# Attention and routing reordered by hand as a software pipeline, diagonal rows on ScalarE, prefix counts on TensorE

## The chip, the cores and the metric

The kernel runs on one core of a Trainium2 chip. The core has five engines with an instruction queue each, which work in order and wait for each other through semaphores: TensorE (PE, matmuls; its weight loads are listed as PEld), VectorE (DVE), ScalarE (ACT), GpSimd (POOL), and SyncE (SP), which here only issues DMAs. The metric is the device time of one execution, in microseconds (us); lower is better.

## The reference, cut to what matters

Inputs are float32: r, k, v of shape (4, 8, 768, 48) (batch, heads, time, head width), decays w and bonus u of (8, 48), eight expert embeddings, a temperature tau, and expert weights w1 (8, 384, 1024) and w2 (8, 1024, 384).

```
for t in range(768):                        # attention, for each batch and head
    y[t]  = r[t] @ (state + outer(u * k[t], v[t]))
    state = w[:, None] * state + outer(k[t], v[t])
x = y as 3072 rows of 384                   # row = batch * 768 + t, all heads side by side
logits = (x / |x|) @ (emb / |emb|).T / tau  # 8 experts
e = argmax(logits); gate = softmax(logits)[e]
out[row] = gate * (relu(x[row] @ w1[e]) @ w2[e])
```

## The kernel before, in words

The time axis is cut in 6 chunks of 128 steps. A chunk of one batch is a unit: 24 units, taken chunk by chunk, the 4 batches of a chunk in turn. Four units make a group, which is routed together.

For one unit (`attend`, L211 to L275) GpSimd scales K into the padded tile Kpad by powers of the decay (L220), and forms KU, the product K * u * R (L222, L223); VectorE sums KU over each head to diag (L225); GpSimd multiplies V by diag to xd, the diagonal term (L227). TensorE transposes R (L231) and Kpad (L236), two heads at a time, into PSUM; VectorE brings R out, scaled, as RT (L233), and ScalarE brings K out as KT (L238). TensorE multiplies KT by RT for all head pairs (L244); VectorE masks the result to AT (L248). TensorE then sums into one PSUM tile the part from the carried state (L255, not in the first chunk) and AT times V (L258); VectorE adds xd to get the rows X (L264). TensorE makes the new state part (L269, not in the last chunk), VectorE adds it to the state (L273) and GpSimd decays the state (L274). A float32 matmul stands in the trace as two instructions, a transpose as one.

For one group (`route`, L332 to L399) ScalarE squares and sums each X (L345), TensorE transposes X (L348), ScalarE brings it out (L350), and TensorE multiplies it by the embeddings (L352). Some twenty small VectorE instructions find the first maximal expert and the gate. Running counts are made on VectorE (`pre`, L378 to L381), and two small matmuls turn them into each row's place in its expert's list (L383, L384). Then SyncE writes the rows to DRAM (L395), and GpSimd writes each row's number into the list with four indirect DMAs, the scatters (L396). The four write the same tensor, so each waits until the one before has landed.

After the last group, SyncE reads the lists back (L409), GpSimd gathers rows (L422), and for each expert TensorE transposes 512 rows (L438) and runs the two matmuls (L444, L449). This part is the same code in both kernels.

The order of each engine's instructions is not as written: a list scheduler places them by its own cost estimates. All PSUM tiles come from one pool of 8 banks, and tiles such as Kpad rotate among 3 buffers. The experts' embeddings are prepared, and the decays' range is checked (`decays`, with the instruction L150), before the first unit.

Of the kernel before, what the change touches and what calls it, by code (L numbers as in the profile page):

```python
# [9 lines left out]
F32 = mybir.dt.float32  # L10
# [8 lines left out]
N = B * S  # L19
C = 128  # L20
# [12 lines left out]
WAKE = 7  # L33
# [6 lines left out]
def build_first(k):  # L40


    nc, pool = k.nc, k.const
    wc = pool.tile([128, NP], F32, name="wc")
    nc.vector.memset(wc, 1.0)
    with nc.allow_non_contiguous_dma(reason="384 words"):
        for s in range(2):
            q = nc.sync if s == 0 else nc.scalar
            q.dma_start(out=wc[s * DP : s * DP + D, :], in_=k.w.rearrange("(p s) d -> s d p", s=2)[s])
    k.ones = pool.tile([128, 128], F32, name="ones")  # L50
    nc.vector.memset(k.ones, 1.0)
    wide = k.aconst.tile([128, 512], F32, name="wide")
    nc.vector.memset(wide, 1.0)
    ps = k.ps.tile([128, 512], F32, name="ps", tag="ps")
    for _ in range(WAKE):
        nc.tensor.matmul(ps, k.ones, wide, start=True, stop=True)
    k.ident = pool.tile([128, 128], F32, name="ident")
    make_identity(nc, k.ident)

    for lst, name, count in ((k.Rpad, "Rpad", 6), (k.Kpad, "Kpad", 3)):  # L60
        for i in range(count):
            t = k.aconst.tile([128, H, DP], F32, name=f"{name}{i}")
            nc.gpsimd.memset(t[:, :, D:DP], 0.0)
            lst.append(t)
    step = k.aconst.tile([128, NP, C], F32, name="step")
    seed = k.aconst.tile([128, NP, C], F32, name="seed")
    nc.gpsimd.memset(seed, 0.0)
    nc.gpsimd.memset(seed[:, :, 0:1], 1.0)
# [4 lines left out]
    nc.vector.tensor_copy(step, wc[:, :, None].to_broadcast([128, NP, C]))  # L73
    nc.vector.memset(step[:, :, 0:1], 0.0)
    t = k.aconst.tile([128, NP, C], F32, name="wpow")
    flat = lambda a: a.rearrange("q p i -> q (p i)")
    nc.vector.tensor_tensor_scan(flat(t), flat(step), flat(seed), 0.0, ALU.mult, ALU.add)
    mid = k.aconst.tile([128, NP], F32, name="mid")
    nc.vector.reciprocal(mid, t[:, :, C // 2])
    k.rpow = k.aconst.tile([128, NP, C], F32, name="rpow")  # L80
    kp = k.aconst.tile([128, NP, C], F32, name="kp")
    over_i = mid[:, :, None].to_broadcast([128, NP, C])
    nc.vector.tensor_mul(kp, t[:, :, ::-1], over_i)
    ps = k.ps.tile([128, NP, 2, DP], F32, name="ps", tag="ps")
    for p in range(NP):
        nc.tensor.transpose(ps[:, p].rearrange("q s d -> q (s d)"), kp[:, p, :], k.ident)
    k.kpow = k.aconst.tile([128, H, D], F32, name="kpow")
    nc.vector.tensor_copy(k.kpow.rearrange("q (p s) d -> q p s d", s=2), ps[:, :, :, 0:D])
    nc.vector.tensor_mul(k.rpow, t, over_i)
    wC = k.aconst.tile([128, NP], F32, name="wC")  # L90
    nc.vector.tensor_mul(wC, t[:, :, C - 1], wc)
    k.wC = wC[:, :, None].to_broadcast([128, NP, D])
# [10 lines left out]
def build_consts(k):  # L103
# [9 lines left out]
    nc.sync.dma_start(  # L113
        out=k.u_bc.rearrange("p h d -> p (h d)"),
        in_=bass.AP(tensor=k.u.tensor, offset=k.u.offset, ap=[[0, 128], [1, DM]]),
    )
    for b in range(B):
# [7 lines left out]
    k.ebase = numbers(k, "ebase", [128, E], [[N, E]], 0, 0)  # L125
# [8 lines left out]
def empty_lists(k):  # L134
    k.nc.sync.dma_start(out=k.list.rearrange("(p n) o -> p (n o)", p=128), in_=k.none)
    k.nc.vector.memset(k.cum, 0.0)


def decays(k):

    nc, pool = k.nc, k.const
    wrow = k.aconst.tile([1, DM], F32, name="wrow")
    nc.sync.dma_start(out=wrow, in_=k.w.rearrange("(o h) d -> o (h d)", o=1))
# [10 lines left out]
def build_experts(k):  # L154

    nc, pool = k.nc, k.aconst
    emb = pool.tile([E, DM], F32, name="emb")
    nc.sync.dma_start(out=emb, in_=k.emb)
    tau = pool.tile([E, 1], F32, name="tau")
    nc.sync.dma_start(out=tau, in_=bass.AP(tensor=k.tau.tensor, offset=k.tau.offset, ap=[[0, E], [1, 1]]))  # L160
# [8 lines left out]
    ps = k.ps.tile([128, NK, E], F32, name="ps", tag="ps")  # L169
# [19 lines left out]
def load(k, i, other=None):  # L189

    nc = k.nc
    other = other or nc.sync
# [8 lines left out]
    other.dma_start(out=R[:, :, 0:D], in_=of(k.r))  # L201
# [9 lines left out]
def attend(k, i):  # L211
# [4 lines left out]
    K, R, V = k.loaded.pop(i)  # L216
    T = k.state[b]

    Kw = k.Kpad[i % len(k.Kpad)]
    nc.gpsimd.tensor_mul(Kw[:, :, 0:D], K, k.kpow)  # L220
    KU = k.work.tile([128, H, D], F32, name="KU", tag="KU")
    nc.gpsimd.tensor_mul(KU, K, k.u_bc)  # L222
    nc.gpsimd.tensor_mul(KU, KU, R[:, :, 0:D])  # L223
    diag = k.work.tile([128, H], F32, name="diag", tag="diag")
    nc.vector.reduce_sum(diag, KU, axis=AX.X)  # L225
# [3 lines left out]
    rt = k.ps.tile([128, NP, C], F32, name="ps", tag="ps")  # L229
# [4 lines left out]
    kt = k.ps.tile([128, NP, C], F32, name="ps", tag="ps")  # L234
# [5 lines left out]
    at = [k.ps.tile([128, NP, C], F32, name="ps", tag="ps") for _ in range(2)]  # L240
    for p in range(NP):
        for s in range(2):
            rows = slice(s * DP, s * DP + D)
# [386 lines left out]
```

## Time and profile before

| | us |
|---|---|
| median of 3 runs (755.43 to 757.86) | 755.45 |
| the profiled execution | 752.4 |
| its span, first to last instruction | 750.5 |
| first transposes of the first unit start | 29.87 |
| first transposes of the first expert start | 386.27 |
| TensorE busy, share of the span | 86% |
| mean granted TensorE clock, share of full speed | 0.742 |

Start times are counted from the span's start. The profile also says at which clock TensorE ran: 0.50 is 1.2 GHz and 1.00 is 2.4 GHz, its two levels. An engine's idle time is listed with what ended it, as in "[0.68 <-ACT KT L238]": idle for 0.68 us, until the ScalarE instruction of line 238 on tile KT was done. A matmul's end is modelled and includes time in which the next already runs, so that the distance from start to start is the better measure.

### The profile page before, as it was taken

The page shows a single profiled execution, that of the slowest core. Times are in us where ns is not written, and L with a number is a line of the kernel's source. Part 1 is how long each engine was busy: PE and PEld are TensorE (multiplying, and loading weights), DVE is VectorE, ACT ScalarE, POOL GpSimd, SP SyncE. Part 2 cuts the span into 40 slices and gives each one's busy share as a digit, 9 for nine tenths or more (in the row PEclk, how much of TensorE's full clock was granted, in tenths as well). Part 3 has the DMA queues.
Part 4 walks back from the last instruction along what each step waited for, and adds up shares of the span by engine and source line. Part 5 has one row for each costly group of instructions (what it writes and reads, how often), then busy time and mean ns, then how long its engine had stood idle before and what let it go on. Part 6 is the DMA issues. An engine that isn't in the chain of part 4 may idle for free.

```text
span 750.5 us, 6703 instructions
## 1 busy us (share of the span) xinstructions
PE 647.1 (86%) x2536; PEld 460.3 (61%) x2536; DVE 168.0 (22%) x414; ACT 80.8 (11%) x169; POOL 213.3 (28%) x282
## 2 busy tenths in 40 slices
PE   4388897899899899898039999999999999999991
PEld 2378887798798798788024545555454555545450
DVE  3533332323333223324010111202011110202000
ACT  1011110100101101102002010010201011010200
POOL 5653352554344242220240211203031221302010
PEclk8555555555555555557559999999999999999996
DMA  9354654313313210100120333424132333300000
GB/s 184 63 149 107 122 94 119 84 32 64 74 33 64 58 26 11 42 1 1 43 62 0 129 100 105 129 84 140 20 136 87 127 109 105 125 1 31 1 30 5
DMA packets 95565, 54.39 MB, mean 72 GB/s; under 512 B 78558, under 2 KB 90175, under 8 KB 95523
## 3 DMA queue, kind: packets, MB, share of 16 engines
q1 hardware_dynamic: 89410, 44.19, 22.9%
q0 software_dynamic: 4864, 9.48, 4.2%
q8 instruction: 22, 0.36, 0.2%
q10 hardware_dynamic: 1248, 0.20, 0.1%
q14 instruction: 21, 0.16, 0.1%
HBM read 45.86 MB, written 11.13 MB: 76 GB/s over the span
## 4 chain that ended last, share of the span: by engine, by line
PE 75%; issue 9%; DMA 4%; POOL 3%; DVE 2%; ACT 2%; SPq 0%; POOLq 0%; DVEq 0%; ACTq 0%
PE ps L444 23%; PE ps L449 22%; PE ps L258 8%; PE ps L244 5%; PE ps L269 4%; DMA list<-token,posi 3%; PE ps L255 3%; PE ps L352 3%; PE ps L231 2%; PE ps L236 2%; PE ps L348 1%; PE ps L438 1%; ACT KT L238 1%; POOL list L396 1%; DVE AT L248 0%
## 5 line engine op out<-in xcount | busy, mean ns | idle before, releaser
L444 PE MATMUL ps<-xTe,w 128*128 128x512 f32 x384 | 168.9, 601 | 0.4 <-DVE xTe L439 0.4
L449 PE MATMUL ps<-w,hT 128*128 128x384 f32 x512 | 166.4, 486 | 0.0
L449 PEld LDWEIGHTS ps<-w,hT 128*128 128x128 f32 x512 | 97.5, 190 | 69.3 <-issue 3.8
L444 PEld LDWEIGHTS ps<-xTe,w 128*128 128x128 f32 x384 | 73.3, 193 | 91.5 <-issue 84.8
L452 POOL DMA_INDIRECT out_dram<-y,take x32 | 32.4, 1011 | 270.2 <-DVE y L451 266.0
L258 PE MATMUL ps<-V,AT 128*128 128x48 f32 x384 | 85.6, 396 | 6.5 <-DVE AT L248 6.5
L258 PEld LDWEIGHTS ps<-V,AT 128*128 128x128 f32 x384 | 84.7, 323 | 8.0 <-DVE AT L248 8.0
L451 DVE TENSOR_SCALAR y<-ps,G 128x384 f32<-128x384 f32 x32 | 19.8, 618 | 298.5 <-PE ps L449 298.5
L445 ACT ACTIVATE hT<-ps 128x512 f32<-128x512 f32 x64 | 38.2, 597 | 319.6 <-PE ps L444 319.6
L244 PE MATMUL ps<-RT,KT 48*128 48x128 f32 x384 | 49.0, 431 | 16.5 <-ACT KT L238 16.5
L244 PEld LDWEIGHTS ps<-RT,KT 48*128 48x128 f32 x384 | 42.1, 320 | 26.0 <-ACT KT L238 26.0
L220 POOL TENSOR_TENSOR Kpad<-K,kpow 128x384 f32<-128x384 f32 x24 | 23.9, 1000 | 87.4 <-PE ps L269 79.9
L269 PE MATMUL ps<-V,Kpad 128*128 128x96 f32 x160 | 44.2, 437 | 0.0
L248 DVE TENSOR_TENSOR AT<-ps,umask 128x512 f32<-128x512 f32 x48 | 30.9, 686 | 50.5 <-PE ps L244 50.5
L396 POOL DMA_INDIRECT list<-token,posi x24 | 24.3, 1014 | 56.9 <-DMA list<-token,posi 46.6
L422 POOL DMA_INDIRECT G<-xs,take x32 | 32.6, 1017 | 26.0 <-PE ps L444 9.9
L255 PE MATMUL ps<-state,RT 128*128 128x96 f32 x160 | 39.5, 427 | 0.0
L269 PEld LDWEIGHTS ps<-V,Kpad 128*128 128x128 f32 x160 | 38.5, 334 | 0.0
L255 PEld LDWEIGHTS ps<-state,RT 128*128 128x128 f32 x160 | 34.8, 321 | 4.4 <-issue 4.2
L264 DVE TENSOR_TENSOR X<-ps,xd 128x384 f32<-128x384 f32 x24 | 13.4, 558 | 99.4 <-PE ps L258 98.3
L352 PEld LDWEIGHTS ps<-ent,xT 128*128 128x128 f32 x144 | 30.5, 314 | 5.2 <-ACT xT L350 5.1
L352 PE MATMUL ps<-ent,xT 128*128 128x8 f32 x144 | 30.1, 337 | 2.9 <-ACT xT L350 2.8
(113 smaller groups left out, 440.8 us busy)
## 6 DMA issues: line engine op xcount, KB each, us to landing
w<-in_moe_w_dram SPq DMA_DIRECT2D x16, 1536.0 KB
xs<-X SPq DMA_DIRECT2D x24, 192.5 KB
K<-in_k_dram SPq DMA_DIRECT2D x24, 192.0 KB
V<-in_v_dram SPq DMA_DIRECT2D x24, 192.0 KB
Rpad<-in_r_dram SPq DMA_DIRECT2D x23, 192.0 KB
G<-xs,take POOLq DMA_INDIRECT x32, 3.2
out_dram<-y,take POOLq DMA_INDIRECT x32, 2.6
list<-token,posi POOLq DMA_INDIRECT x24, 4.8
```

The lines of the kernel that those rows point to most:

```text
L244: mm(at[s][:, p, :], KT[rows, p, :], RT[rows, p, :], start=True, stop=True)
L248: nc.vector.tensor_mul(a, at[s], k.umask[:, None, :].to_broadcast([128, NP, C]))
L255: mm(pair(y, p), RT[:, p, :], T[:, p, :], start=first, stop=False, skip_group_check=True)
L258: mm(y[:, h, :], AT[h % 2][:, h // 2, :], V[:, h, :], start=first, stop=(h == H - 1), skip_group_check=True,)
L269: mm(st[:, p, :], pair(Kw, p), pair(V, p), start=True, stop=True)
L352: mm(lg[:, b, :], xT[:, m, :], k.ent[:, m, :], start=(m == 0), stop=(m == NK - 1))
L396: nc.gpsimd.indirect_dma_start(out=k.list[:, :], out_offset=IndirectOffsetOnAxis(ap=posi[:, b : b + 1], axis=0), in_=k.token[:, c, b : b + ...
L422: nc.gpsimd.indirect_dma_start(out=G[:, :], out_offset=None, in_=k.xs[:, :], in_offset=IndirectOffsetOnAxis(ap=take, axis=0), bounds_check ...
L444: mm(ps[:, 0:n], w1[:, m, f * 128 : (f + 1) * 128], xT[:, m, 0:n], start=(m == 0), stop=(m == NK - 1))
L445: nc.scalar.activation(hT[:, f, 0:n], ps[:, 0:n], ACT.Relu)
L449: mm(ps, hT[:, f, t * 128 : (t + 1) * 128], w2[:, f, :], start=(f == 0), stop=(f == NF - 1))
L452: nc.gpsimd.indirect_dma_start(out=k.out[:, :], out_offset=IndirectOffsetOnAxis(ap=take, axis=0), in_=y[:, :], in_offset=None, bounds_chec ...
```

## The change

The attention part is put under a manual schedule: each engine now runs its instructions in the order in which they are written. `attend` and `route` are cut into steps, and a new function `attention` writes in iteration i the steps of several units: transposes of unit i+1, scaling for unit i+2, sums of unit i, scores of unit i+1, transposed rows of unit i-1, logits of unit i-2, and for a group the choice of expert and the ranks 3 iterations, and places, row write and scatters 4 iterations after its last unit.

The diagonal rows xd move from one GpSimd instruction to eight ScalarE instructions, one for each head. The running counts on VectorE are replaced by three more small matmuls with the matrix of ones. The experts' embeddings are prepared in iteration 1 and the decays' range is checked in iteration 4, their DMAs issued by ScalarE. Seven wake-up matmuls become 6 before and 4 after the first transposes. The decay powers are made by four short scans, unit 0's Kpad by VectorE. Kpad rotates among 4 buffers, PSUM banks are given out by kind of tile, and a group's rows are one tile, written to DRAM by one DMA.

```diff
+def own_rows(k, i):
+    diag, V = k.diag.pop(i), k.loaded[i][2]
+    for h in range(H):
+        k.nc.scalar.mul(xd[:, h, :], V[:, h, :], diag[:, h : h + 1])
-    nc.gpsimd.tensor_mul(xd, V, diag[:, :, None].to_broadcast([128, H, D]))
...
+def ranks(k, g):
+    g.rank = k.ps.tile([128, B, E], F32, name="rank", tag="st")
+    mm(g.rank, k.umask, g.oh, start=True, stop=False)
+    for b in range(1, B):
+        mm(g.rank[:, b:B, :], k.ones, g.oh[:, 0 : B - b, :], start=False, stop=False, skip_group_check=True)
+    mm(g.rank, k.ones, k.cum[:, None, :].to_broadcast([128, B, E]), start=False, stop=True)
-    for b in range(1, B):
-        nc.vector.tensor_add(pre[:, b, :], pre[:, b - 1, :], oh[:, b - 1, :])
-    mm(rank, k.umask, oh, start=True, stop=False)
-    mm(rank, k.ones, pre, start=False, stop=True)
...
+    for i in range(-1, units + 5):
+        if 0 < i + AHEAD < units:
+            load(k, i + AHEAD)
+        if i in (B, 2 * B):
+            load_weights(k, i // B - 1, k.weights[i // B - 1])
+        whole(places, i - 4)
+        whole(put, i - 4)
+        on(own_rows, i)
+        on(turn, i + 1)
+        on(scaled, i + 2)
+        on(own, i + 1)
+        on(states, i)
+        of_group(squares, i - 1)
+        whole(choose, i - 3)
+        on(sums, i)
+        on(carry, i)
+        on(rows, i)
+        on(scores, i + 1)
+        on(own_sum, i + 1)
+        of_group(turn_rows, i - 1)
+        of_group(logits, i - 2)
+        whole(ranks, i - 3)
+        whole(gates, i - 3)
+        if i == 1:
+            build_experts(k)
+        if i == B:
+            decays(k)
...
+        return self.pool.tile(shape, dtype, name=name, tag=tag, bufs={"tp": 2, "at": 2}.get(tag, 1))
...
+    with ExitStack() as ctx1, tc.manual_schedule():
```

TensorE at the start, before: `kp` is the decay power, `emb` the embeddings, `Rpad` the padded R.

```order
L86 MATMUL ps<-ident,kp 128x128 x4
L171 MATMUL ps<-ident,emb 128x8 x3
L231 MATMUL ps<-ident,Rpad_106 128x128 x4
L236 MATMUL ps<-ident,Kpad_118 128x128 x4
L244 MATMUL ps<-RT,KT 128x128 x8
```

The same place after; `wake` is the result of the wake-up matmuls, which nothing reads.

```order
L84 MATMUL kpT<-ident,kp 128x128 x4
L60 MATMUL wake<-wide,ones 128x512 x4
L252 MATMUL rt<-ident,Rpad_119 128x128 x4
L257 MATMUL kt<-ident,Kpad_111 128x128 x4
L270 MATMUL at<-RT,KT 128x128 x8
```

The embedding transposes no longer stand ahead of the first unit, and four wake-up matmuls do.

TensorE in a unit of a middle chunk, before:

```order
L231 MATMUL ps<-ident,Rpad_116 128x128 x4
L236 MATMUL ps<-ident,Kpad_122 128x128 x4
L244 MATMUL ps<-RT,KT 128x128 x8
L255 MATMUL ps<-state_177,RT 128x96 x4
L258 MATMUL ps<-V,AT_680 128x48
L269 MATMUL ps<-V,Kpad_122 128x96 x3
```

And after, where `rt`, `kt`, `st`, `y`, `at`, `xp`, `lg` are the PSUM tiles of the two transposes, the state part, the sums, the scores, the transposed rows and the logits:

```order
L252 MATMUL rt<-ident,Rpad_119 128x128 x4
L257 MATMUL kt<-ident,Kpad_117 128x128 x4
L287 MATMUL st<-V,Kpad_115 128x96 x4
L317 MATMUL y<-state_195,RT 128x96 x4
L320 MATMUL y<-V,AT_732 128x48
...
L270 MATMUL at<-RT,KT 128x128 x8
L411 MATMUL xp<-ident,X 128x128 x3
L426 MATMUL lg<-ent,xT 128x8 x3
```

Before, the scores (L244) follow the transposes of the same unit; after, the state part and all sums of the unit before stand between the two, and the routing's matmuls are spread over the units.

GpSimd around the scatters of a group, before:

```order
L396 DMA list<-token,posi 24576x1 x2
L223 TENSOR_TENSOR KU<-KU,Rpad_110 128x384
L220 TENSOR_TENSOR Kpad_122<-K,kpow 128x8x48
L227 TENSOR_TENSOR xd<-V,diag 128x384
L274 TENSOR_TENSOR state_175<-state_175,wC 48x4x48 x2
L396 DMA list<-token,posi 24576x1 x2
```

After:

```order
L304 TENSOR_TENSOR state_195<-state_195,wpow 48x4x48 x2
L457 TENSOR_TENSOR ssq<-ssq,half 128x4
L486 DMA list<-token,posi 24576x1 x4
L219 TENSOR_TENSOR Kpad_113<-K,kpow 128x8x48
L227 TENSOR_TENSOR KU<-K,u_bc 128x384
L228 TENSOR_TENSOR KU<-KU,Rpad_121 128x384
```

The four scatters now stand in one block, and the scaling of K for the unit after next (L219) stands behind them.

## Rows read from the trace of the kernel before

**Rows 1.** The page, 40 slices of the span: busy tenths, granted clock in tenths.

```profile
PE   4388897899899899898039999999999999999991
PEclk8555555555555555557559999999999999999996
```

**Rows 2.** Busy time by stretch: length, PE, PEld, DVE, ACT, POOL, clock, DMA share, GB/s.

```profile
10.30:29.80 19.50, 0.35 (x3) 0.35 (x3) 7.63 (x17) 0.62 (x2) 17.07 (x19) 0.55 0.57 118
...
190.90:247.97 57.07, 52.04 (x265) 49.08 (x265) 18.09 (x50) 6.85 (x17) 24.60 (x33) 0.50 0.27 56
...
359.00:386.20 27.20, 0.28 (x1) 0.17 (x1) 0.41 (x2) 0.00 (x0) 6.39 (x7) 0.50 0.09 23
```

**Rows 3.** Timeline of the start: start, us, engine, line, operation, [idle before].

```profile
1.62 8.19 PE L56 MATMUL ps<-wide,ones 128*128 128x512 f32 x14 [1.62 <-DVE cum L136]
...
26.04 2.97 DVE L150 TENSOR_TENSOR far<-lohi 1x1 f32<-1x1 f32 x1
...
29.45 0.48 PE L171 MATMUL ps<-ident,emb 8*128 8x8 f32 x3 [19.20 <-DVE far L151]
...
29.87 1.11 PE L231 MATMUL ps<-ident,Rpad 128*128 128x128 f32 x4
```

**Rows 4.** Timeline of TensorE in one unit of a middle chunk.

```profile
204.17 2.08 PE L244 MATMUL ps<-RT,KT 48*128 48x128 f32 x16 [0.68 <-ACT KT L238]
206.18 2.02 PE L255 MATMUL ps<-state,RT 128*128 128x96 f32 x8
...
213.97 1.06 PE L236 MATMUL ps<-ident,Kpad 128*128 128x128 f32 x4
215.71 0.58 PE L244 MATMUL ps<-RT,KT 48*128 48x128 f32 x2 [0.68 <-ACT KT L238]
```

**Rows 5.** Timeline of TensorE in the last two units and the last routing.

```profile
339.66 2.02 PE L255 MATMUL ps<-state,RT 128*128 128x96 f32 x8
...
341.83 1.08 PE L231 MATMUL ps<-ident,Rpad 128*128 128x128 f32 x4
...
345.91 1.16 PE L244 MATMUL ps<-RT,KT 48*128 48x128 f32 x16 [0.73 <-ACT KT L238]
347.00 1.13 PE L255 MATMUL ps<-state,RT 128*128 128x96 f32 x8
...
352.62 2.02 PE L352 MATMUL ps<-ent,xT 128*128 128x8 f32 x12
```

**Rows 6.** Busy time by stretch around the end of attention (columns of Rows 2).

```profile
343.50:353.50 10.00, 9.20 (x86) 8.49 (x85) 4.43 (x10) 3.43 (x9) 0.78 (x1) 1.00 0.01 2
353.70:355.70 2.00, 0.94 (x5) 0.84 (x5) 1.75 (x9) 0.00 (x0) 0.06 (x1) 0.50 0.00 0
```

**Rows 7.** Timeline from the last group's first scatter to the first expert.

```profile
358.89 1.06 POOL L396 DMA_INDIRECT list<-token,posi  x1 [1.56 <-DVE posi L391]
...
373.68 0.97 POOL L396 DMA_INDIRECT list<-token,posi  x1 [3.34 <-DMA list<-token,posi]
...
386.27 0.88 PE L438 MATMUL ps<-ident,G 128*128 128x128 f32 x3 [4.28 <-DMA G<-xs,take]
```

**Rows 8.** All 24 scatters: from issue to landing.

```profile
DMA to landing us min/median/max: 3.0/4.8/8.5
```

**Rows 9.** Timeline while the first group's scatters and expert weights are under way.

```profile
86.22 1.21 POOL L396 DMA_INDIRECT list<-token,posi  x1 [0.86 <-DVE posi L391]
...
94.97 0.97 POOL L396 DMA_INDIRECT list<-token,posi  x1 [7.54 <-DMA list<-token,posi]
...
116.80 0.66 PE L258 MATMUL ps<-V,AT 128*128 128x48 f32 x2 [3.44 <-DVE AT L248]
```

**Rows 10.** Groups by line and shape: count, busy us, mean ns, idle before.

```profile
L220 POOL TENSOR_TENSOR Kpad<-K,kpow 128x384 f32<-128x384 f32 x24 | 23.9, 1000 | 87.4 <-PE ps L269 79.9 <-DVE kpow L88 5.4 <-PE ps L236 2.0
...
L238 ACT COPY KT<-ps 128x512 f32<-128x512 f32 x24 | 14.0, 585 | 70.8 <-PE ps L236 70.8
...
L370 ACT ACTIVATE l<-l 128x32 f32<-128x32 f32 x6 | 1.4, 229 | 16.0 <-DVE oh L365 16.0
```

More of the change, by code (lines that the diff above doesn't have):

```diff
@@ L53, in build_first, with wake @@
     nc.vector.memset(wide, 1.0)
[L54 to L57, printed above, removed]
+    k.ident = k.const.tile([128, 128], F32, name="ident")
     make_identity(nc, k.ident)
-    for lst, name, count in ((k.Rpad, "Rpad", 6), (k.Kpad, "Kpad", 3)):
+    def wake(count):
+        ps = k.ps.tile([128, 512], F32, name="wake", tag="y")
+        for _ in range(count):
+            nc.tensor.matmul(ps, k.ones, wide, start=True, stop=True)
@@ L238, in attend, with scores @@
     nc.scalar.copy(KT, kt)
-    at = [k.ps.tile([128, NP, C], F32, name="ps", tag="ps") for _ in range(2)]
+    k.RT[i], k.KT[i] = RT, KT
+def scores(k, i):
+    nc = k.nc
+    RT, KT = k.RT[i], k.KT.pop(i)
+    at = [k.ps.tile([128, NP, C], F32, name="at", tag="at") for _ in range(2)]
     for p in range(NP):
@@ L317, in recur, with recurred @@
             nc.sync.dma_start(out=k.x_dram[:, bass.ds(t0, TS), :], in_=ys)
[L320 removed]
+def recurred(k, c):
     nc = k.nc
[L322 to L323 removed]
+    g = group(k, c)
     Q, W = 4, D // 4
[L325 to L329 removed]
@@ new lines, in recurred, with group, over_e @@
+    for b in range(B):
+        src = k.x_dram.rearrange("(q b h) s e -> b q s h e", q=Q, b=B)[b]
+        dst = g.X[:, b, 0:DM].rearrange("p (h q e) -> q p h e", q=Q, e=W)
+        for q in range(Q):
+            nc.sync.dma_start(out=dst[q], in_=src[q, c * C : (c + 1) * C])
+    return g
+def group(k, c):
+    g = Net()
+    g.c = c
+    g.X = k.rows.tile([128, B, ROW], F32, name="X", tag="X")
+    g.ssq = k.rt.tile([128, B], F32, name="ssq", tag="ssq")
+    g.xT = {}
+    return g
+def over_e(a):
+    return a[:, :, None].to_broadcast([128, B, E])
@@ new lines, in turn_rows, with squares @@
+def turn_rows(k, g, b):
+    nc = k.nc
+    X = g.X[:, b, 0:DM]
+    xp = k.ps.tile([128, NK, C], F32, name="xp", tag="xp")
+    for m in range(NK):
+        nc.tensor.transpose(xp[:, m, :], X[:, m * 128 : (m + 1) * 128], k.ident)
+    g.xT[b] = k.work.tile([128, NK, C], F32, name="xT", tag="xT")
+    nc.scalar.copy(g.xT[b], xp)
+def squares(k, g, b):
+    sq = k.work.tile([128, DM], F32, name="sq", tag="sq")
+    k.nc.scalar.activation(sq, g.X[:, b, 0:DM], ACT.Square, accum_out=g.ssq[:, b : b + 1])
@@ new lines, in put, with route, attention, on @@
+            in_=k.token[:, g.c, b : b + 1], in_offset=None, bounds_check=E * N - 1, oob_is_err=False,
+        )
+def route(k, g):
+    for b in range(B):
+        squares(k, g, b)
+        turn_rows(k, g, b)
+        logits(k, g, b)
+    for step in (choose, ranks, gates, places, put):
+        step(k, g)
+def attention(k):
+    units = B * NCH
+    def on(f, i):
+        if 0 <= i < units:
+            f(k, i)
+    def of_group(f, i):
+        if 0 <= i < units:
+            f(k, k.groups[i // B], i % B)
+    def whole(f, i):
+        if 0 <= i < units and i % B == B - 1:
+            f(k, k.groups[i // B])
+    for i in range(-1, units + 5):
[25 more added lines that the diff above has]
+            decays(k)
```

319 lines of the change are left out of this document (168 added, 151 removed).

## The prediction, made before the changed kernel ran

> **What bounds the kernel now.** I read the page's slices first, then busy time by stretch, then the timeline of one unit. The slices show two programs: attention up to about 357 us, in which TensorE is busy for eight or nine tenths at the low clock, and the experts from 386 us, where it is full at the high one [rows 1]. Between them lie 27 us in which it does nothing, and at the start 19.5 us with 0.35 us of work [rows 2]. So attention is bound by TensorE at 1.2 GHz, its two ends by chains of waits, the experts by TensorE. A group of four units takes 57.07 us and holds 52.04 us of TensorE work [rows 2]: better order alone has 5 us a group to win. The clock has much more.
>
> At the start TensorE waits 19.20 us for embeddings that only the routing needs: VectorE makes them behind a check that takes 2.97 us [rows 3]. In a unit the one regular wait is 0.68 us for the K copy, in 11.54 us from scores to scores [rows 4].
>
> **What the clock does.** From start to start, the 16 instructions of the scores take 2.01 us at the low clock [rows 4] and 1.09 us at the high one [rows 5], a ratio of 0.54. It rose twice in this part: during the wake-up matmuls, and near 343.4 us, in a stretch that holds L255 and transposes and no wait [rows 5, 6]. It fell near 353.7 us although TensorE was busy, with matmuls of 8 columns [rows 5, 6]. So being busy is not enough; the kind of instruction counts, and wide ones without a wait are what went before a rise. After the change 8 transposes, 8 instructions of L287 and 8 of L317 follow each other in every unit with no result to wait for: at the low clock about 5 us, where before the scores' wait cut the row. I therefore expect the clock to rise within one or two units of dense work.
>
> The Trainium skill says otherwise of a third of that stretch: "TensorE: Matmul & The Clock Gate", section "Part 4: PE-mode transpose", has it that transposes do not count for the clock as matmuls do. By that rule the stretch may not suffice, which is the low-clock rival below. The trace speaks against its strict form, since four transposes of L231 stand ahead of the rise near 343.4 us.
>
> **The change part by part.** Times are starts in the profiled execution.
>
> *Start.* The embeddings leave the path. The wake-up chain ran from 1.62 to 9.81 us with 14 instructions [rows 3]; 12 end near 8.6, then the four transposes of the powers and 8 more wake-up instructions. These cost 4.7 us at the chain's mean of 0.585 and about half of that if all run at the high clock; I take 4. Unit 0's transposes start at 13.1 instead of 29.87 us. I cost the four scans and unit 0's Kpad at nothing, since the wake-up matmuls cover them; uncovered they are 1 to 2 us.
>
> *A unit.* At the low clock: 11.54 us, less 0.9 for the wait and its restart, plus 9 routing instructions at 0.21 to 0.25 (L255: 8 in 2.02 with its tail), is 12.5 us. At the high clock 12.5 x 0.54 = 6.8 us; 5.8 in the first chunk, which lacks L317. GpSimd keeps per unit the scaling of K, 1.0 us [rows 10], KU and the state; with xd and the scatters it was busy for 24.60 us a group, at most 6.2 a unit, and VectorE for 18.09, 4.5 a unit [rows 2], so both hide beside TensorE's 6.8. ScalarE gets eight of 48 columns for xd: between 0.229 us (32 columns) and 0.585 us (512 columns) each [rows 10], I take 0.25, 2 us a unit. That hides beside TensorE's 6.8; at the upper end, 4.7 plus the copies and squares, ScalarE would just become the bound (1 us a unit). The three further rank matmuls cost 1 us a group; the VectorE counts they replace hid in its idle time, and leaving them out wins nothing.
>
> *To the first scatters.* 13.1 plus 2.8 for the first transposes, K copy and scores is 15.9. Four units of 5.8 plus 2 for the embeddings in iteration 1 make 41.1; three of 6.8, the check of 2.97 us and 1 for the ranks make 65.5 us at iteration 7.
>
> *The new wait.* In iteration 7 and every fourth after it, GpSimd holds four scatters in a row. Each waits for the landing of the one before, and behind them stands the scaling of K that TensorE needs one iteration later. Before, two scatters were followed by four or more other instructions, and still a block on GpSimd once cost TensorE 3.44 us [rows 9]. Four issues took 358.89 to 373.68 us, 14.8 us for three waits [rows 7]; the median landing of all 24 is 4.8 us [rows 8], so this holds in the middle too. Places are ready about 2 us into the iteration, then 14.8, the last issue 1.0 and the scaling 1.0 [rows 7, 10]: TensorE's next transposes of K come at 18.8 us, while its own iteration took 6.8 to 12.5. It idles 6 to 12 us, and the clock falls.
>
> After that: the rest of one unit at the low clock, 11.6 us; of the next, 4.5 us low and (12.5 - 4.5) x 0.54 = 4.3 high; one unit of 6.8. A group is 18.8 + 11.6 + 8.8 + 6.8 = 46.0 us against 57.07. Four groups are 184; plus 6, since the first collides with the second expert's weights (8.75 us from issue to issue [rows 9]), less 3 for the last chunk without L287: 187. Iteration 23 starts at 252.5 us.
>
> *The end of attention.* GpSimd now holds eight scatters with a landing wait at each. Group 4's start 2 us into iteration 23 and leave the queue at 17.8. Only then can it take the root of the last group's squares; root, gate and places took less than 4.25 us before (L352 ends at 354.64, first scatter at 358.89 [rows 5, 7]); I take 3.7, plus 0.5 for the last landing. So the last four start at 22.0, and from there to the first expert it is 386.27 - 358.89 = 27.4 us [rows 7]. Experts start at 252.5 + 49.4 = 301.9 us.
>
> *Experts.* The same instructions, TensorE full: no change.
>
> **The sum.** 386.27 - 301.9 = 84.4 us less. The profiled execution took 752.4 us, 1.9 of it outside the span of 750.5: 668.0. The median of the three runs shown lies 3.05 above it, so I forecast 671 us for the median.
>
> **The rivals.** *High clock nearly throughout.* The idle stretch does not bring the clock down, or it rises at once. A group is 18.8 + 6.3 + 2 x 6.8 = 38.7 us, four with the same corrections 157.8, experts start at 272.7: 642 us. For it: the clock held for 10 us in the last units although there was a wait of 0.73 [rows 5, 6]. Against: after the wake-up matmuls the mean clock of the 19.5 nearly idle us is 0.55 [rows 2], so it was high for only about the first 2 of them.
>
> *Low clock throughout.* Unit 0 at 16.6, four units of 10.6 plus 2, three of 12.5 plus 4.5: iteration 7 at 103. A group is 18.8 + 11.6 + 2 x 12.5 = 55.4, four 222.6 in all; with 51 for the end the experts start at 376.6: 9.7 us less, 746 us. The order has then won the start and given most of it back at the doubled scatters of the end. For it: over 300 us of dense work at 0.50 [rows 1]. Against: the longer stretch without waits.
>
> *Slower: the scatters land late.* On top of the low clock, 19 landing waits stand on the path, three in each of four groups and seven at the end. From 746 it turns slower than 759 once each takes 0.7 us more than the 4.9 of the tail, that is 5.6. At 6.7, about what the spread from the median 4.8 to the maximum 8.5 has in its middle [rows 8], it is 34 us more: 780 us. For it: the group's rows and more loads now move at the same time. Against: the median.
>
> The Trainium skill has a rule for this rival: "SBUF — State Buffer", section "SBUF: two separate sides", says that some VectorE instructions keep GpSimd from writing a DMA's descriptors. By it denser VectorE work would delay each scatter, to 780 us. The trace shows no sign: three waits in the tail, with VectorE idle, took 14.8 us, no less than three at the median landing.
>
> **How the numbers follow.** About 0.5% (3.8 us) is what a measurement of this kernel can tell from no change: 751.7 to 759.2 us. Chances: the forecast, 650 to 705 us, 0.52; high clock, 0.22; low clock, 0.16, of which a fifth falls inside 0.5% or slightly above; late scatters, 0.10. The forecast's own range comes from where the clock rises: in the first unit after each wait takes 5.5 us off a group, 22 in all (649 us), in the third it adds 5.7, 23 in all (694). The range for 8 in 10 goes from 632, below the high clock's 642, to 742, just short of the low clock's. Faster by over 0.5%: 0.85; within: 0.06; slower: 0.09.
>
> **What would show it.** Right: the first transposes near 13 us; a granted clock over 0.5 in most of attention between the scatters; TensorE idle before L257, ended by GpSimd's L219, once a group for 6 to 12 us and at no other place for long; eight scatters in a row before the experts, which start near 302. Wrong: the clock at 0.50 all along, or no wait at L257, or the wait on ScalarE's copy behind the eight xd instructions. The forecast fails by its largest term if the clock stays low, and by some 5 us a group if the scatters' chain is shorter than 14.8 us.

## The result, and the profile after

The changed kernel takes 669.9 us (median; single executions 666.2, 669.8, 670.0 and 694.1), the kernel before 755.4. The ratio is 0.889, 95% interval 0.877 to 0.902: faster, 1 us beside the forecast of 671. Over all of the runs below, single executions of the kernel before took from 736.5 to 757.9 us. Medians here are over all executions; ratios leave out those taken as disturbed, so that a kernel with many of these has a median and no ratio. The profiled execution took 669.8 us, its span 668.0.

The slices of the page, busy tenths and the granted clock in tenths:

```profile
PE   8699349669479297007999999999999999999990
PEclk9799757958879578556999999999999999999995
```

Beside [rows 1]: the experts begin in slice 19 of 16.7 us, where it was slice 21 of 18.8, and the clock of attention is no longer 5 throughout: it falls and rises. Busy time by stretch: the start, the way to the first iteration with four scatters, the four groups from there, the end, each cut within 0.3 us of an iteration's first instruction (length, PE, PEld, DVE, ACT, POOL, granted clock, DMA share, GB/s):

```profile
0.00:12.20 12.20, 10.57 (x25) 4.87 (x26) 5.88 (x18) 1.28 (x1) 6.84 (x30) 1.00 1.02 167
12.20:65.60 53.40, 47.64 (x447) 45.39 (x445) 32.31 (x73) 23.85 (x84) 30.32 (x38) 0.90 0.83 172
65.60:119.50 53.90, 34.98 (x273) 33.67 (x272) 17.31 (x46) 13.75 (x49) 20.95 (x25) 0.72 0.55 118
119.50:167.30 47.80, 34.78 (x272) 33.47 (x272) 17.19 (x46) 13.75 (x49) 20.83 (x25) 0.75 0.38 67
167.30:210.50 43.20, 29.88 (x272) 28.70 (x272) 17.20 (x46) 13.63 (x49) 20.80 (x25) 0.84 0.34 60
210.50:253.90 43.40, 31.27 (x246) 29.95 (x245) 14.97 (x39) 13.74 (x49) 16.77 (x18) 0.72 0.06 19
253.90:301.90 48.00, 9.26 (x63) 8.83 (x62) 7.34 (x40) 4.23 (x16) 11.57 (x12) 0.57 0.12 38
```

A middle group took 57.07 us with 52.04 of TensorE work at 0.50 [rows 2]. Now it takes 43.2 to 53.9, with 30 to 35 of work and the rest idle: the work got shorter by the clock, and a hole came. The waits of TensorE name it (us in all, times, longest):

```profile
PE kt L257 <- POOL Kpad L219: 56.5, 4, 18.7
PE ps L558 <- DVE rowf L556: 31.4, 1, 31.4
PE ps L583 <- DMA G<-xs,take: 6.5, 3, 4.3
PE ps L179 <- DVE emb L176: 3.9, 1, 3.9
PE at L270 <- ACT KT L259: 1.9, 3, 0.7
```

The 0.68 us wait for the K copy in every unit [rows 4] has gone but for 1.9 us at the start, and the 19.20 us for the embeddings [rows 3] are 3.9. New are four waits at L257. The timeline of the first (start, us, engine, line, operation, idle before):

```profile
65.60 0.63 PE L252 MATMUL rt<-ident,Rpad 128*128 128x128 f32 x4
...
67.58 1.19 POOL L486 DMA_INDIRECT list<-token,posi  x1 [4.16 <-DVE cum L478]
...
72.67 0.64 PE L252 MATMUL rt<-ident,Rpad 128*128 128x128 f32 x4
...
76.48 0.97 POOL L486 DMA_INDIRECT list<-token,posi  x1 [7.71 <-DMA list<-token,posi]
...
84.49 0.97 POOL L486 DMA_INDIRECT list<-token,posi  x1 [7.04 <-DMA list<-token,posi]
...
89.94 0.97 POOL L486 DMA_INDIRECT list<-token,posi  x1 [4.48 <-DMA V<-in_v_dram]
90.93 1.01 POOL L219 TENSOR_TENSOR Kpad<-K,kpow 128x384 f32<-128x384 f32 x1
91.99 1.11 PE L257 MATMUL kt<-ident,Kpad 128*128 128x128 f32 x4 [18.68 <-POOL Kpad L219]
...
103.58 0.67 PE L252 MATMUL rt<-ident,Rpad 128*128 128x128 f32 x2
```

Four scatters, each behind the landing of the one before, and K's scaling behind all four. (For the fourth the view names a load of V as what ended the wait: this trace lacks the landing times of 15 of the 24 scatters, these among them.) It is read backwards: L257, in the iteration that began at 72.67, waits for L219, and L219 began the moment L486 left GpSimd. After it the four transposes take 1.11 us, the low clock's time, against 0.60 at the high one; the rest of that unit lasts to 103.58. The end of attention:

```profile
258.90 1.05 POOL L486 DMA_INDIRECT list<-token,posi  x1 [15.70 <-DVE new L477]
...
275.34 1.03 POOL L486 DMA_INDIRECT list<-token,posi  x1 [2.33 <-DVE new L477]
...
289.70 0.97 POOL L486 DMA_INDIRECT list<-token,posi  x1 [3.27 <-DMA list<-token,posi]
```

Eight scatters in a row where there were four [rows 7]; the first expert begins at 301.95 instead of 386.27.

### The profile page after: what moved, and what is told of

Its sections match the earlier page's. It is cut to its first block, busy times and chain, and to the rows that moved or that the text cites. A ratio compares the mean times of both kernels' runs of the same rounds, so it can differ in the third digit from the quotient of the medians.

```text
span 668.0 us, 6921 instructions
## 1 busy us (share of the span) xinstructions
PE 545.0 (82%) x2578; PEld 367.4 (55%) x2578; DVE 156.6 (23%) x393; ACT 122.5 (18%) x361; POOL 190.6 (29%) x233
## 3 DMA queue, kind: packets, MB, share of 16 engines
q1 hardware_dynamic: 88944, 43.98, 26.6%
## 4 chain that ended last, share of the span: by engine, by line
PE 52%; issue 2%; DMA 1%; DVE 0%; POOL 0%; POOLq 0%
PE ps L589 25%; PE ps L594 25%; PE ps L583 2%; DMA G<-xs,take 1%; DMA list<-token,posi 0%; DVE xTe L584 0%; DVE y L596 0%; DVE need L613 0%; POOL G L567 0%; DVE some L624 0%; DVE some L625 0%; DVE flag L627 0%; POOLq L567 0%; DVE count L610 0%; DVE need L615 0%
## 5 line engine op out<-in xcount | busy, mean ns | idle before, releaser
L596 DVE TENSOR_SCALAR y<-ps,G 128x384 f32<-128x384 f32 x32 | 19.8, 618 | 298.5 <-PE ps L594 298.5
L257 PE MATMUL kt<-ident,Kpad 128*128 128x128 f32 x96 | 18.3, 324 | 56.5 <-POOL Kpad L219 56.5
L242 ACT ACTIVATE xd<-V,diag 128x48 f32<-128x48 f32 x192 | 45.8, 321 | 83.8 <-DVE diag L234 83.8
L486 POOL DMA_INDIRECT list<-token,posi x24 | 23.9, 994 | 114.2 <-DMA list<-token,posi 75.1
L320 PE MATMUL y<-V,AT 128*128 128x48 f32 x384 | 50.9, 290 | 0.0
L320 PEld LDWEIGHTS y<-V,AT 128*128 128x128 f32 x384 | 50.1, 211 | 0.0
L257 PEld LDWEIGHTS kt<-ident,Kpad 128*128 128x128 f32 x96 | 13.9, 169 | 57.4 <-POOL Kpad L219 57.4
L567 POOL DMA_INDIRECT G<-xs,take x32 | 32.7, 1021 | 25.5 <-issue 15.6
L274 DVE TENSOR_TENSOR AT<-at,umask 128x512 f32<-128x512 f32 x48 | 30.9, 686 | 16.4 <-PE at L270 16.3
L270 PE MATMUL at<-RT,KT 48*128 48x128 f32 x384 | 31.3, 308 | 1.9 <-ACT KT L259 1.9
L304 POOL TENSOR_TENSOR state<-state,wpow 48x192 f32<-48x192 f32 x40 | 20.4, 511 | 37.2 <-DVE state L300 32.7
L234 DVE TENSOR_REDUCE diag<-KU 128x8 f32<-128x384 f32 x24 | 13.1, 545 | 65.3 <-POOL KU L228 65.3
L270 PEld LDWEIGHTS at<-RT,KT 48*128 48x128 f32 x384 | 26.3, 208 | 3.6 <-ACT KT L259 2.4
L287 PE MATMUL st<-V,Kpad 128*128 128x96 f32 x160 | 25.8, 316 | 0.9 <-DVE at L471 0.9
L287 PEld LDWEIGHTS st<-V,Kpad 128*128 128x128 f32 x160 | 24.5, 234 | 1.9 <-DVE at L471 1.9
```

Of the source, the lines that this page charges most:

```text
L242: k.nc.scalar.mul(xd[:, h, :], V[:, h, :], diag[:, h : h + 1])
L270: nc.tensor.matmul(at[s][:, p, :], KT[rows, p, :], RT[rows, p, :], start=True, stop=True)
L274: nc.vector.tensor_mul(a, at[s], k.umask[:, None, :].to_broadcast([128, NP, C]))
L287: nc.tensor.matmul(st[:, p, :], pair(Kw, p), pair(V, p), start=True, stop=True)
L320: mm(y[:, h, :], AT[h % 2][:, h // 2, :], V[:, h, :], start=first, stop=(h == H - 1), skip_group_check=True,)
L486: nc.gpsimd.indirect_dma_start(out=k.list[:, :], out_offset=IndirectOffsetOnAxis(ap=g.pos[:, b : b + 1], axis=0), in_=k.token[:, g.c, b : ...
```

## The experiments

The theory: TensorE's clock is the main gain, and the block of four scatters is what the change leaves on the table. The rivals: order alone, or the single edits (xd on ScalarE, counts on TensorE, embeddings later). The kernel before, run beside them, took 741.8 us (median) beside e1 to e4, 753.7 beside c1, e5_fill, e6 and e7, and 741.9 beside the others, so ratios are compared, or traces.

**The changed kernel again (c1_changed_again), no edit.** 

> The changed kernel itself, unaltered, beside the others of this call: what the single edits are to be compared with. In e1_spread and e3_vector_counts, whose code is the changed kernel's up to 65 us, the clock rose for good only at 46.3 us against 35.3 in the profile of the changed kernel, and iteration 7 began at 70 instead of 65.6. If that is chance, this kernel shows it too: 666 to 690 us, iteration 7 between 65 and 70 us. If not, 670 us and the rise at 35.

Measured: 680.4 us, four from 676.9 to 697.2; ratio 0.910 (0.893 to 0.927). Iteration 7 began at 65.5 us as before, the experts at 309.2 instead of 301.9: the clock stayed low from 216.1 us to the end of attention, where it had risen once more in the first profile (0.72 in the stretch from 210.5). So two executions of one program differ by 7 us, of which the waits at L257, 58.4 us instead of 56.5, are 1.9 and the clock most of the rest; a single edit worth less can't be told from the time.

**Clock without the order (e4_before_warm).**

```
+    warm = k.ps.tile([128, 512], F32, name="ps", tag="ps")
+    for _ in range(2):
+        mm(warm, k.ones, k.wide, start=True, stop=True)
     at = [...]                    # the scores, in the kernel before
```

> The kernel before, its order untouched, with two matmuls of 128x512 a unit whose result nobody reads, between K's transposes and the scores (where TensorE waits 0.68 us for the K copy). At the low clock they are 1.7 us a unit. Theory (the gain of the change is mostly TensorE's clock): the clock rises in the first units and stays up in most of attention, a unit takes 7 to 9 us, bounded by GpSimd with its landing waits; 655 us (635 to 690). Rival (the gain is the order, the gaps it closes): the clock may rise but falls again at the waits, 700 to 740 us. Rival (these matmuls do nothing for the clock): 24 units by 1.0 us more, 779 us.

Measured: 685.1 us, ratio 0.924 (0.919 to 0.929). TensorE got more work and the kernel became 7.6% shorter. Its busy time from 65.7 to 190 us (columns as above):

```profile
65.70:190.00 124.30, 106.15 (x694) 87.09 (x695) 44.94 (x131) 15.15 (x39) 61.12 (x84) 0.80 0.39 79
```

A clock of 0.80 where it was 0.50, units of 6.5 to 16.6 us, experts at 324.4 us instead of 386.3, with the start (first unit at 29.3) and, but for the two matmuls, TensorE's order untouched; the scheduler moved some of GpSimd's instructions. The theory holds: beside its own runs of the kernel before it wins 57 us by the median, 7.6%, where the whole change wins 11.1% in its first runs and 9.0% in c1_changed_again. So most of the change's gain is to be had by the clock alone. The rival that wide matmuls do nothing is out. Its 779 us were priced too low: the pair took 1.8 us at the high clock and up to 3.5 at the low one, not 1.7. The pair also fills the 0.68 us wait for the K copy, so whether its width or the closed gap raised the clock is not told apart.

**One scatter an iteration (e1_spread), and the root ahead of it (e6_spread_root).**

```
-    for b in range(B): nc.gpsimd.indirect_dma_start(...)     # in put
...
+    whole(root, i - 2)                 # e6 only; gates() lost its pow
     on(carry, i)
+    spread(k, i - 2 * B + 1)           # scatter b of the group, all groups but the last
```

> The changed kernel with one scatter an iteration (behind the state's scaling on GpSimd, in the four iterations that follow the places) in place of four in a row; only the last group keeps its four together. Theory (the block of four in front of K's scaling causes the once-a-group idle time, and the idle time the clock's falls): the 56.5 us of waits at L257 go, TensorE's clock stays at 1.00 from its first rise to the tail, iterations 7 to 23 take 4 x (4 x 6.8 + 1) = 113 us instead of about 188, the tail with its eight scatters stays: 595 us (585 to 610). Rival A (the clock falls anyway, as the matmuls of 48 rows follow): only the idle time goes, 613 us or more, and low stretches stay. Rival B (the landings simply move: each scatter waits in its own iteration, and GpSimd becomes the bound of every unit): 640 to 670 us, with short waits at L257 in every iteration.

Measured: 625.9 us, four from 615.7 to 633.5, beside 739.7 to 757.0 for the kernel before. The waits of TensorE in it:

```profile
PE ps L571 <- DVE rowf L569: 31.8, 1, 31.8
PE st L287 <- DVE at L471: 11.1, 4, 7.4
```

The wait at L257 is gone, so the block was its cause; rival B (GpSimd the bound of every unit) is out. But the forecast of 595 missed, and rival A came true in its number and its low stretches (613 us or more), whatever brings them. The clock fell at 100.9 and 179.4 us, the first time 0.5 us into a new wait of 7.4 us:

```profile
102.30 1.00 POOL L492 DMA_INDIRECT list<-token,posi  x1 [0.28 <-POOL state L304]
103.37 1.04 POOL L457 TENSOR_TENSOR ssq<-ssq,half 128x4 f32<-128x4 f32 x1
104.44 0.97 DVE L458 TENSOR_SCALAR ssq<-ssq 128x4 f32<-128x4 f32 x1 [4.81 <-POOL ssq L457]
...
107.77 2.02 PE L287 MATMUL st<-V,Kpad 128*128 128x96 f32 x8 [7.38 <-DVE at L471]
```

There the group's root (L457) stood on GpSimd behind a scatter waiting for its landing, VectorE waited for the root, and TensorE for VectorE. e6_spread_root moves the root.

> e1_spread with the root of the squares on GpSimd ahead of the iteration's scatter, and one iteration earlier. In e1_spread the root stood behind a scatter that waited for the landing of the one before; VectorE waited up to 9.6 us for it, TensorE 7.4 us for VectorE, and the clock fell. Theory: that wait goes and with it the falls of the clock before the tail; iterations 7 to 23 take 4 x 28.5 = 114 us (135 in e1_spread), 600 us (588 to 615). Rival (the clock falls in e1_spread for the long weight loads or for the matmuls' kind): 615 to 626 us, low stretches stay at the same places.

Measured: 615.2 us, four from 604.8 to 625.9, ratio 0.816 (0.781 to 0.851): faster than both kernels and the lowest median found, though its executions overlap those of e1_spread. It lies at the border of the theory (588 to 615) and the rival (615 to 626). The wait at L287 is down to 2.8 us in four, the iteration that held the longest to 13.2 us from 19.3, yet the clock still fell, at 93.6 and 131.1 us. So the fall in e1_spread did not need its wait of 7.4 us. Around the first fall:

```profile
88.00:93.50 5.50, 5.50 (x58) 5.32 (x56) 3.03 (x8) 2.29 (x8) 4.04 (x5) 1.00 0.79 143
93.80:98.00 4.20, 3.76 (x18) 3.36 (x18) 2.85 (x13) 2.89 (x12) 2.63 (x5) 0.50 0.65 103
```

TensorE was busy without a gap up to 93.5 us. What stood there were the scores (48 rows), matmuls of 8 columns and the group's five rank matmuls (from 92.5); a wait of 0.44 us came only at 96.1, after the fall. The next two runs ask whether that narrow row is the cause.

**Counts on VectorE (e3_vector_counts; e10_spread_vector_counts on top of e6).**

```
+    g.pre = ...; for b in range(1, B): nc.vector.tensor_add(g.pre[:, b, :], g.pre[:, b - 1, :], oh[:, b - 1, :])
...
-    for b in range(1, B): mm(g.rank[:, b:B, :], k.ones, g.oh[:, 0 : B - b, :], ...)
-    mm(g.rank, k.ones, k.cum[:, None, :]..., ...)
+    mm(g.rank, k.ones, g.pre, start=False, stop=True)
```

> The changed kernel with a group's counts made on VectorE again (one copy, four adds a group) and two rank matmuls instead of five. Theory (hidden on both engines): 670 us, within 2 us. Rival (the VectorE chain delays the places and so the scatters): each group's scatters 1 to 2 us later, 675 to 680 us. Rival (the three matmuls cost on the path): 665 us.

Measured: 687.9 us, ratio 0.929 (0.920 to 0.938), interval overlapping that of c1_changed_again. The first scatter of a group comes 2.6 instead of 2.0 us into the iteration, and TensorE waits 3.6 us at L287 in four, where it was 0.9. The experts begin 17.2 us later than in the changed kernel's profile. Of these, 4.5 stand in the first 65 us, whose code is the same (the clock rose at 46.3 instead of 35), and 9.4 in iterations 19 to 22, where the clock stayed low as in c1_changed_again. Inconclusive; a cost of a few us is likely, not shown.

> e6_spread_root with a group's counts on VectorE, so that three narrow matmuls of the ranks (24, 16 and 8 columns, 0.8 us) are gone. In e6_spread_root the clock fell at 93.6 us with no wait before it, in a row of scores (48 rows), matmuls of 8 columns and the five rank matmuls. Theory (the narrow row is what brings the clock down): with less of it the falls in iterations 11 and 15 become rarer, 595 to 610 us; rival (something else does): the falls stay at the same places, 605 to 625 us.

Measured: 635.0 us, four from 619.7 to 643.7. The falls did not become rarer (77.8, 118.7 and 190.4 us), and the longer VectorE chain made TensorE wait 7.0 us at L287. It lies outside both ranges and speaks neither for nor against the narrow row.

**Another order in the iteration (e8_best_order; e9_best_early with the embeddings first).**

```
         on(turn, i + 1)
+        of_group(logits, i - 2)        # was behind turn_rows
...
         on(states, i)
...
+        whole(ranks, i - 3)            # was behind logits; now in the xp bank
         on(sums, i)
...
+        whole(places, i - 3)           # was i - 4;  choose: i - 2, was i - 3
```

> e6_spread_root with another order inside the iteration: the logits between K's transposes and the state matmuls, the ranks between state and sums (in the xp bank), the choice one iteration earlier, the places and the group's first scatter in the ranks' iteration. So no narrow matmul stands beside the scores any more, and the last groups' scatters begin one iteration earlier. Theory (the narrow row behind the scores brings the clock down, the number of scatters at the end sets the tail): no fall of the clock before the tail, iteration 23 at 178 to 182 us (190 in e6_spread_root), the tail 45 to 50 us instead of 56: 588 us (578 to 600). Rival (the falls have another cause): low stretches stay, 600 to 615 us. Rival (VectorE's new place makes TensorE wait): waits of 0.5 us or more at L287 or L317 in every group.

Measured: 648.9 us, four from 634.0 to 655.3, ratio 0.879 (0.869 to 0.890): slower than e6_spread_root. The theory of 588 us fell, and its last rival came true in kind: VectorE's new place makes TensorE wait, though at L426 and not at L287 or L317. The logits' bank is read by the choice that now stands at the iteration's end on VectorE:

```profile
PE lg L426 <- DVE l L441: 9.4, 5, 2.3
```

The clock fell in each of the four groups at its ranks (67.5, 101.7, 135.8, 176.8 us), and an iteration with ranks took 13 to 15 us.

> e8_best_order with the embeddings and the range check ahead of the loop, as in e7_embeddings_first, where the first unit began 1.2 us later but TensorE had no wait in iteration 1 and the clock rose at 28.8 us instead of 35 to 58. Theory: iteration 4 at 38 to 39 us in every run, the time e8_best_order's or up to 6 us less, with less spread. Rival (the clock's rise is chance in both): no difference beyond the spread of the runs.

Measured: 653.8 us, four from 630.1 to 668.6, ratio 0.886 (0.874 to 0.897). Iteration 4 began at 40.6 us (38 to 39 forecast; 48.9 in e8_best_order) and the clock was at 1.00 from 5.3 to 59.9, which it was in no other run. But the time was not less, nor the spread: four falls at the ranks gave it back, as in e8_best_order.

**xd back on GpSimd (e2_pool_rows).**

```
-    for h in range(H): k.nc.scalar.mul(xd[:, h, :], V[:, h, :], diag[:, h : h + 1])
+    k.nc.gpsimd.tensor_mul(xd, V, diag[:, :, None].to_broadcast([128, H, D]))
```

> The changed kernel with the diagonal rows xd back on GpSimd as one instruction a unit (0.83 us in the kernel before) instead of eight on ScalarE. Theory (the move to ScalarE is hidden either way; only where xd stands behind the four scatters does it add its own length to the wait at L257): +0.83 us in each of four groups, and up to as much again for the X row behind it: 673 us (669 to 678). Rival (GpSimd has no room for it): +0.8 us in most of 24 units and longer waits, 690 us or more. Rival (ScalarE's eight instructions held the path): faster than the changed kernel, 655 to 665 us.

Measured: 696.6 us, ratio 0.944 (0.935 to 0.954), apart from c1_changed_again's interval: slower by far more than xd's 0.85 us. The timeline of its end:

```profile
279.35 1.05 POOL L485 DMA_INDIRECT list<-token,posi  x1 [14.52 <-DVE new L476]
...
293.52 0.96 POOL L485 DMA_INDIRECT list<-token,posi  x1 [4.25 <-DMA list<-token,posi]
294.50 0.85 POOL L241 TENSOR_TENSOR xd<-V,diag 128x384 f32<-128x384 f32 x1
295.38 0.56 DVE L332 TENSOR_TENSOR X<-y,xd 128x384 f32<-128x384 f32 x1 [15.78 <-POOL xd L241]
...
303.78 1.05 POOL L485 DMA_INDIRECT list<-token,posi  x1 [6.02 <-DVE new L476]
```

The last unit's xd stands behind group 4's four scatters, and its rows wait 15.78 us for it. In the changed kernel those rows are made beside the scatters (X at 259.05, first scatter at 258.90). But there too the last group's root stands behind the four scatters (at 271.95), so that the last four begin 16.4 us after group 4's first; here it is 24.4 (279.35 to 303.78). So xd's place costs 8 us at the end. Another 10.6 us stand before iteration 7 (at 76.2 instead of 65.6), where the clock rose at 57.7 us; as it rose at 58.5 in e5_fill, whose code is the changed kernel's up to there, xd's part in that is not shown. What ScalarE gives is a queue without landing waits.

**The embeddings first (e7_embeddings_first).**

```
+    build_experts(k)
+    decays(k)
     for i in range(-1, units + 5):
...
-        if i == 1: build_experts(k)
-        if i == B: decays(k)
```

> The changed kernel with the embeddings and the check of the weights' range ahead of the first unit again, as in the kernel before. Theory (the start's 17.7 us come from this alone): TensorE waits for the embeddings, the first unit begins at 27 to 30 us instead of 12.2, and the 3.9 us of wait in iteration 1 go: 10 to 16 us more than the changed kernel, 680 to 686 us. Rival (the shorter start is from the scans and the wake-up's order): the first unit at 14 to 18 us, within 4 us of the changed kernel.

Measured: 668.8 us, ratio 0.897 (0.883 to 0.910): nothing lost. The theory fell. One row of the kernel before and two of this one:

```profile
24.76 0.58 POOL L164 TENSOR_TENSOR emb_nrm<-emb_nrm,half 8x1 f32<-8x1 f32 x1
```

```profile
10.31 0.58 POOL L172 TENSOR_TENSOR emb_nrm<-emb_nrm,half 8x1 f32<-8x1 f32 x1 [4.86 <-DVE cum L147]
...
13.42 0.65 PE L252 MATMUL rt<-ident,Rpad 128*128 128x128 f32 x4
```

In the kernel before the root stood on GpSimd behind the scalings and products of several units, and the check of 2.97 us [rows 3] on VectorE before its use. In a written order that holds the embeddings' steps first, TensorE has them at 13.2 us. The first unit begins 1.2 us later than without and holds a wait of 2.2 us for the check, but iteration 1 has no wait of 3.9 us. Iteration 7 begins at 65.0 us, against 65.6.

**TensorE busy through the wait (e5_fill, e5b_fill_half).**

```
     for p in range(NP): nc.tensor.transpose(rt[:, p, :], pair(R, p), k.ident)
+    if i > 2 * B and i % B == 1:
+        k.fill(28)                     # 14 in e5b; matmuls of 128x512, never read
```

> The changed kernel with 28 matmuls of 128x512, whose result nobody reads, put between R's and K's transposes in the one iteration of each group in which TensorE waits for K's scaling: the wait stays (11.9 us of such work at the high clock fit in it), TensorE is only no longer idle. Theory (the idle time costs twice, the second time through the clock): the clock stays at 1.00 through the wait, 7.3 us less in each of four groups: 641 us (630 to 655). Rival (only the idle time costs, the clock falls for another reason): the changed kernel's own time within 8 us. Rival (the filling overruns the wait): some us more than the changed kernel.

Measured: 690.6 us, ratio 0.917 (0.889 to 0.946). My size was wrong: the 28 took 24.2 us, and the wait was overrun.

```profile
84.72 24.20 PE L60 MATMUL wake<-wide,ones 128*128 128x512 f32 x56
108.75 0.60 PE L260 MATMUL kt<-ident,Kpad 128*128 128x128 f32 x4
```

But the clock stayed at 1.00 from 58.5 to 287.2 us, through the places of all four waits and through the rank matmuls of the five groups before the last. From K's transposes to the second unit after them took 12.7 us (108.75 to 121.43) in three groups and 10.9 in the fourth; in the changed kernel it is 19.8, 19.7, 14.7 and 17.2.

> e5_fill with 14 instead of 28 matmuls of 128x512 in the wait. In e5_fill the 28 took 24.2 us at the high clock, 0.86 us each and not the 0.43 that its expectation was worked out from, and overran the wait by 6 us and more; its clock stayed at 1.00 from 58 to 287 us. 14 take 12.1 us, just the shorter waits. Theory: the group keeps the wait and loses the low stretch behind it, 7 us a group against the changed kernel (from K's transposes to the next unit 6.1 us instead of 11.6, and 1.6 in the unit after): 28 us less in all than the changed kernel where it starts alike, 640 to 655 us. Rival (the clock's fall costs nothing, the wait hides it): within 8 us of the changed kernel's 670 to 680.

Measured: 664.5 us, ratio 0.900 (0.893 to 0.906), above the 640 to 655. The same stretches took 14.5, 14.4, 16.9 and 15.9 us, 9.7 less in sum than in the changed kernel. Waits of 7.7, 2.4 and 1.2 us were left behind the filling in three groups; the clock fell once in each group, in the longest of these waits or within 0.4 us after one of 0.9 to 2.4 us. So the low clock behind a wait costs 5.6 us a group when it is wholly avoided ((71.4 - 48.9) / 4, with e5_fill's four stretches), not the 7 that I had put on it; the idle time itself, 12 to 19 us, is the larger part, as e1_spread showed.

## Why the prediction was right

*The start.* First transposes forecast at 13.1 us, measured at 12.2. The number held, its reason only half: "the embeddings leave the path" is not needed, as e7_embeddings_first shows. What went, by the rows of both, is the order in which GpSimd and VectorE had them queued; the scans and the wake-up's order changed with it and were not run apart.

*To iteration 7.* 65.5 forecast, 65.60 measured, and that is luck: two misses of about 3.6 us cancel. Iteration 4 began at 44.8 us instead of 41.1, since the wait for the embeddings was 3.9 us instead of 2 and the clock was low from 25.1 to 35.3 us, which I had left out. From there to iteration 7 it took 20.8 us instead of 24.4, since the check (2.97 us) cost TensorE nothing. High units took 5.7 to 6.6 where I had 5.8 and 6.8. xd on ScalarE took 1.91 us in eight (2 forecast). In the first chunk the K copy stood behind it twice and TensorE waited 0.61 us each time, which it did not in e2_pool_rows; later it delayed nothing.

*The new wait.* At the place, once a group, four times, and no other of that size in attention. K's transposes came 26.4, 20.5, 20.8 and 19.6 us after the start of the iteration with the scatters; forecast were 24.8 for the first and 18.8. Then the unit's rest at the low clock: 11.6 forecast; 11.6, 11.6, 8.1 and 9.9 measured. Then 8.8 forecast; 8.2, 8.1, 6.6 and 7.4. The last unit, 6.8 forecast, took 7.7 in three groups, for their ranks, which I had counted in the first alone. The waits' 1 to 2 us too little and the low stretches' up to 3.5 too much cancel, again by luck: four groups 187 forecast, 188.6 measured (65.60 to 254.17).

*The clock.* It rose 15.0, 14.8, 4.2 and 13.4 us after TensorE resumed; I had put it 4.5 us into the second unit, 16.1. It fell in every wait. That the kind of instruction counts, which the prediction took from the fall near 353.7 us, is not shown: e4_before_warm closed a gap with its wide matmuls, and e8_best_order and e10_spread_vector_counts did not part narrow matmuls from waits. The rival of a low clock throughout failed in the changed kernel and in every run made from it; that of a high one is what e5_fill shows when TensorE isn't left idle. The Trainium skill's rule that transposes don't count for the clock ("TensorE: Matmul & The Clock Gate", section "Part 4: PE-mode transpose") did not keep it from rising in these rows; they hold plain matmuls beside the transposes, so no run here decides the rule.

*The end.* 49.4 us from iteration 23 to the experts forecast, 47.8 measured. Group 4's first scatter left 4.7 us into the iteration, not 2, but the landings were shorter: the last group's first scatter at 21.2 (22.0 forecast), and 26.6 from there to the experts (27.4).

*Late scatters.* They came, but small. The page's middle landing of 4.3 us, against 4.8 [rows 8], rests on 9 scatters of 24, since this trace lacks the other landing times, all of the first group's among them. The issues tell more: from a group's first scatter to its fourth it took 22.4, 16.5, 16.8 and 15.6 us, where I had 20.8 for the first and 14.8. That is why the waits were 1 to 2 us too short in the forecast. In c1_changed_again, whose trace has all 24, the middle landing of the four groups' sixteen is 5.3 us, against 4.9 for the first sixteen of the kernel before. The rival's 6.7 us as a mean did not come: the twelve waits of the four groups took 5.9 us from issue to issue. Whether VectorE has a part, as the Trainium skill's "SBUF — State Buffer", section "SBUF: two separate sides", would have it, no run here decides.

*The sum.* Experts at 301.9 forecast, 301.95 measured. The profiled execution took 669.8 instead of 668.0: the experts needed 366.05 us instead of 364.2, since TensorE waited another 2.2 us for gathered rows after their start, where it was 0.6 before, and the clock rose 9.8 us after it instead of 8.4. That the total came within 1 us is luck beyond the terms: the same program gave 680 us when it ran again. The 0.5% that I took for the noise of this kernel is too little, as its own 736.5 to 757.9 us show. In the low-clock rival four groups with the stated corrections come to 224.6 us, not 222.6, which changes no chance.

What stays open is what brings the clock down where the scatters are spread. Between iteration 1 and the tail the five spread kernels show 15 falls. All stand between 2 us ahead of a group's first rank matmul and 4.3 us behind it; of these kernels' first four rank rows each, 20 in all, 5 passed without a fall. None stands there in the first four rank rows of the changed kernel, its repetition, e5_fill and e7_embeddings_first. Those rows have waits of 0.23 us, the ones with a fall 0.4 to 7.4 us. But a wait alone does not explain it: in e6_spread_root's first fall it came 2.1 us after the fall, and in e3_vector_counts a wait of 0.9 us beside each of the four rows brought none. Narrow row and short wait were not tried apart.

## What to carry to other kernels

When TensorE is busy and its clock is at the lower level, ask for the clock first: two wide matmuls a unit, whose result nobody reads, won 7.6% of the time, where the whole new order won 9 to 11%. A scatter that must wait for the landing of the one before belongs behind everything on its queue that another engine wants soon, one at a time; here four together held the queue for 16 to 22 us, and a low stretch of the clock came after it. And before crediting an edit with a gain, run it alone: the embeddings' place was worth nothing, xd's place on another queue 8 us at the end of attention.

## What the runs showed of the hardware

The same instructions without a wait were granted different clocks in executions of kernels that differ only in later code. The stretch from 36 to 46 us, whose code is one and the same, in the changed kernel, in e1_spread and in e5_fill:

```profile
36.00:46.00 10.00, 10.00 (x104) 9.65 (x103) 6.33 (x13) 4.14 (x15) 7.71 (x10) 1.00 0.79 265
```

```profile
36.00:46.00 10.00, 10.00 (x56) 9.69 (x55) 3.07 (x6) 3.49 (x12) 3.72 (x5) 0.50 0.64 212
```

```profile
36.00:46.00 10.00, 10.00 (x56) 9.69 (x55) 3.71 (x7) 2.78 (x11) 3.96 (x5) 0.50 0.52 162
```

TensorE is full in all three. The clock rose at 35, 46 and 58 us, and iteration 7 began at 65.6, 70.8 and 77.2. So 11.6 us of spread are made there, before the first scatter. c1_changed_again, the one program profiled twice, rose at 35 us both times, so no two profiles here show one program at both clocks. The executions of e7_embeddings_first, which has no wait in iteration 1 (rise at 28.8 us), lay within 666.6 to 673.5 us; those of c1_changed_again, beside it, within 676.9 to 697.2.
